# Down-projection of batches 1 to 7 by Strassen's scheme: seven products of quarters, the weights' combinations partly streamed from memory

## The chip, the cores and the metric

The kernel runs on one core of a Trainium2 chip. The metric is the time of one execution in device microseconds (us). A core has a matrix engine (TensorE, in the rows PE; its weight loads are PEld), VectorE (DVE), ScalarE (ACT), GpSimd (POOL) and SyncE (SP), which here issues every DMA. Each engine works through its own instructions in their order, and engines wait for each other on semaphores.

## The reference

```python
def sm_attn(qq, kk, vv):                       # float32 throughout
    s = scale * qq @ kk.T                      # scale = 1/sqrt(64)
    a = exp(s - max(s)); a = a / (sum(a) + 1e-9)
    return a @ vv
p_packed = sm_attn(p, k, v)                    # q, k, v: (8, 8, 576, 64), p: (8, 8, 32, 64)
out = sm_attn(q, p_packed, p_packed)
x = out.transpose(0, 2, 1, 3).reshape(8 * 576, 512)
h = x @ w_in                                   # w_in: (512, 2048)
g = h * tanh(softplus(h))                      # the Mish function
return g @ w_out                               # w_out: (2048, 512)
```

The weights arrive as float64 and are turned into float32 words in the kernel.

## The kernel before

The program handles the eight batches of 576 tokens in turn. Of a batch, 512 tokens ("MAIN") are done in four pieces of 128, and the last 64 ("REST") are kept aside in `g_rest`.

The hidden size 2048 is cut into 16 groups `f` of 128. A group has an *up* part (`Group.up`, matmuls on L707): for each half of the tokens, 288 columns, six matmuls add into a bank `ps_h`. It is six because the values are kept as a high and a low word (`aT_hi`, `aT_lo`, `wp_hi`, `wp_lo`, type fp32r), of which three products are taken, for two halves of the heads. ScalarE applies Mish (`mish`, L728, L730), VectorE splits the result into `g_hi` and `g_lo` (`halves`, L739, L740), and the *down* part (`down_one`, L744 to L746) multiplies it with the matching 128 rows of `w_out`. Its three matmuls (high by high, high by low, low by high) write 512 columns into one of four banks `acc`, once for each 128 tokens. The four banks gather over the 16 groups and are then copied out by ScalarE and VectorE in turn (L751, L753) and stored. The rest tokens of two batches fill one more set of 128 columns, done in `down_rest` (`ps_rest`) through the same lines.

The up weights are not `w_in` itself: `packed_w` multiplies `w_in` by the packed values `ppT` of the batch (L625, a plain float32 product of which TensorE makes two instructions) and splits the result (L636, L637), for 4 groups at a time. All of `w_in` (`wi`) and both words of `w_out` (`wo_hi`, `wo_lo`) stay in SBUF.

The attention of batch b+1 runs beside the projections of batch b, one piece at each `advance`: keys and queries turned (L430), scores (L440, L456 to L460), two exponentials (L468, L301), sums and division (L306 to L315), transposes back and the split (L333 to L339). Batch 0 is different: while it runs, weights are still loaded and converted by ScalarE, GpSimd and VectorE (L594 to L611), and its down-projection is plain float32 (L764).

The order on TensorE is the order of the code. On the other engines it is the code's order up to the end of batch 0 (`by_hand.close()` at `t == NF`); after that a scheduler in the compiler orders them. In the loop, `LAG = 2` puts the down part of a group two groups behind its up part.

Of the kernel before, what the change touches and what calls it, by code (L numbers as in the profile page):

```python
# [13 lines left out]
ALU = mybir.AluOpType  # L14
AX = mybir.AxisListType

LAG = 2
GB = 3
KVB = 8
KQB = 5  # L20
# [3 lines left out]
OB = 2  # L24
ATTENTION = {0: 4, 1: 2}
LOAD0 = 0
LOADS = {0: 1, 2: 1, 4: 1, 5: 1, 6: 1}
LATER = 12
FLOATS = 4
HALFWAY = 8  # L30
SPLIT0 = 14

# [7 lines left out]
def body(  # L40
# [54 lines left out]
    wi = [[const.tile([P, 2, 2, QC], F32, name=f"wi{c}_{g}") for g in range(2)] for c in range(DF // FC)]  # L95
# [4 lines left out]
    wo, wo_hi, wo_lo = {}, {}, {}  # L100

    def wo_slot(dtype, name):
        return wts.tile([P, DO], dtype, name=name, tag="wo", bufs=NF + 1)

    def split_wo(i):
        if i < HALFWAY:
            wo_hi[i], wo_lo[i] = [late[0].tile([P, DO], F32R, name=f"wo_{x}{i}") for x in ("hi", "lo")]
        else:
            wo_hi[i], wo_lo[i] = wo_slot(F32R, "wo_hi"), wo_slot(F32R, "wo_lo")
        both = [  # L110
            nc.scalar.copy(out=wo_hi[i], in_=wo[i]),
            nc.vector.tensor_tensor(out=wo_lo[i], in0=wo[i], in1=wo_hi[i].bitcast(F32), op=ALU.subtract),
        ]
        if i >= NF - SPLIT0:
            for x in both:
                tc.keep_in_program_order(x)
# [53 lines left out]
    class Batch:  # L170
# [12 lines left out]
        def start(self, pool):  # L183
            self.ppT = moe.tile([P, 2, P], F32, name="ppT")
            self.aT_hi = moe.tile([P, 2, S], F32R, name="aT_hi", tag="aT_hi")
            self.aT_lo = moe.tile([P, 2, S], F32R, name="aT_lo")
# [44 lines left out]
        def turn_weights(self, g, pool, by=(None, None)):  # L231
            self.a1T[g] = early.tile([R, 2, NI, P], F32, name="a1T", bufs=2)
# [46 lines left out]
        def match(self, g, pool):  # L279

            s2 = scores(pool, self.ppT[:, g, :], self.qT[g])
            if g == 0:
                self.a2 = moe.tile([P, 2, S // NP, NP], F32, name="a2", tag="aT_hi")
# [26 lines left out]
        def divide(self, gs, half=None):  # L310
# [4 lines left out]
            nc.vector.tensor_tensor(  # L315
# [7 lines left out]
        def back(self, g, halves=1):  # L323
            if self.b or g == 0:
                self.at = att.tile([P, S], F32, name="at", bufs=1)
            else:
                self.at = att.tile([P, S], F32, name="at", tag="T", bufs=2)
# [7 lines left out]
        def upper(self, g):  # L335
            nc.scalar.copy(out=self.columns(self.aT_hi[:, g, :]), in_=self.turned_back(g))

        def lower(self, g):
            nc.vector.tensor_tensor(  # L339
# [7 lines left out]

        def weigh(self, gs):
            self.share(gs)
            for g in range(gs.start, gs.stop):  # L350
                self.back(g)
                self.upper(g)
                self.lower(g)
# [18 lines left out]
    class Later(Batch):  # L372
# [39 lines left out]
        def start(self):  # L412
            self.ppT = moe.tile([P, 2, P], F32, name="ppT")
            self.aT_hi = moe.tile([P, 2, S], F32R, name="aT_hi", tag="aT_hi")
            self.aT_lo = moe.tile([P, 2, S], F32R, name="aT_lo")
# [8 lines left out]
        def pinned(self, x):  # L424
            if self.b == 2:
                tc.keep_in_program_order(x)
# [63 lines left out]
        def values(self, g):  # L490
# [11 lines left out]
            pending.append(lambda: (self.normalize(g, pp_ps), load_next()))  # L502
# [15 lines left out]
        def attention(self):  # L518


            self.by = "ACT" if self.b == 1 else None
            self.start()
            self.kT, self.qT = {}, {}
            for g in range(2):
                self.kT[g] = self.lanes(self.k_t[g])
                load_next()
                yield
            for g in range(2):
                self.score(g)
                yield  # L530
                flush()
                yield
            self.exps()
            for g in range(2):
                self.qT[g] = self.lanes(self.q_t[g])
                load_next()
                yield
            yield from self.turn_weights()
            self.sums(self.exped)
            yield  # L540
            for g in range(2):
                self.values(g)
                yield
            for g in range(2):
                self.turned(g)
            yield
            self.a2 = att.tile([P, 2, S // NP, NP], F32, name="a2", tag="a", bufs=1)
            for g in range(2):
                self.match(g)
                yield  # L550
                flush()
                yield
            both = slice(0, 2)
            self.peak(both)
            yield
            self.rise(both)
            yield
            self.share(both)
            for g in range(2):
                self.back(g)  # L560
                yield
                self.upper(g)
                yield
# [12 lines left out]
    class Weight:  # L576
# [6 lines left out]
        def fetch(self):  # L583
# [5 lines left out]
            self.dst = wi[self.n // 2][self.g][:, self.n % 2].rearrange("p m x -> p (m x)")  # L589
# [23 lines left out]
    class WeightOut(Weight):  # L613
# [3 lines left out]
        def fetch(self):  # L617
            self.st = stg.tile([P, 2 * FC], I32, name="w_st")
            nc.sync.dma_start(out=self.st, in_=w_out_v[:, self.i, :])
            self.dst = wo[self.i] = wo_slot(F32, "wo32")  # L620
# [12 lines left out]
    def part(ps):  # L633
# [405 lines left out]
```

## Time and profile before

| | |
|---|---|
| median of 3 runs | 750.88 us (750.29 to 751.61) |
| the profiled execution | 751.22 us, of which 749.4 us from its first to its last instruction (the span) |
| granted TensorE clock | 0.998 |
| busy: PE, PEld, DVE, ACT, POOL | 733.8, 563.7, 425.4, 296.1, 53.5 us |
| DMA | 56.34 MB, 31.7% of 16 engines' time |
| instructions | 12727 |

The times are microseconds unless ns is written. L744 is line 744 of the kernel. A row of the timeline gives the start, the length, the engine and line, what is written and read, and in brackets an idle time before it with what ended it. A group's row gives its count, its busy time, the mean length of one, and the idle time before them. Lengths of matmuls overlap: two rows that follow each other are read by their starts.

### The profile page before, as it was taken

The numbers are of one execution on the slowest core, as the hardware profiler recorded it, in microseconds if no ns is written. First come the engines' busy times: TensorE is split into PE (matmuls) and PEld (weight loads), VectorE is DVE, ScalarE is ACT, GpSimd is POOL, SyncE is SP. The second block draws the span as 40 slices with busy tenths as digits, with TensorE's granted clock in tenths as the row PEclk, the third lists the DMA queues.
The fourth block names the chain that finished last, engine by engine and source line by source line (L and its number), as shares of the span: only waits on it lengthen the run. The fifth ranks groups of instructions, "written<-read, shape, count | busy, mean of one in ns | idle before, by whom it ended". The sixth has DMA issues, their size and how long they took to land.

```text
span 749.4 us, 12727 instructions
## 1 busy us (share of the span) xinstructions
PE 733.8 (98%) x5160; PEld 563.7 (75%) x5160; DVE 425.4 (57%) x729; ACT 296.1 (40%) x691; POOL 53.5 (7%) x70
## 2 busy tenths in 40 slices
PE   8899999999999999999999999999999999999997
PEld 7545554688787878887787878877788778888886
DVE  3999767765846466554835557372843737332332
ACT  3776746452532433242522514243333424232221
POOL 0485440000000000000000000000000000000000
PEclk9999999999999999999999999999999999999999
DMA  9999960544204440143302342052201100010002
GB/s 235 296 293 247 270 114 1 127 71 95 32 1 111 64 95 1 59 69 72 56 1 80 62 96 32 15 106 41 56 1 42 29 2 1 1 57 1 0 1 71
DMA packets 186602, 56.34 MB, mean 75 GB/s; under 512 B 173488, under 2 KB 175792, under 8 KB 186544
## 3 DMA queue, kind: packets, MB, share of 16 engines
q1 hardware_dynamic: 186544, 55.53, 31.7%
q8 instruction: 41, 0.67, 0.4%
q14 instruction: 17, 0.14, 0.1%
HBM read 46.07 MB, written 9.44 MB: 74 GB/s over the span
## 4 chain that ended last, share of the span: by engine, by line
PE 91%; ACT 4%; DVE 3%; issue 1%; POOL 0%; DVEq 0%; ACTq 0%; POOLq 0%
PE ps_h L707 25%; PE acc L744 15%; PE acc L746 14%; PE acc L745 14%; PE acc L764 6%; PE ps_w L625 4%; PE ps_s L440 3%; PE ps_rest L746 2%; PE ps_rest L745 2%; PE ps_rest L744 2%; PE ps_pp L495 2%; PE ps_warm L828 1%; PE ps_a L482 1%; ACT wround L595 1%; PE ps_h L719 1%
## 5 line engine op out<-in xcount | busy, mean ns | idle before, releaser
L728 ACT ACTIVATE g<-ps_h 128x288 f32<-128x288 f32 (+1 forms) x256 | 97.3, 385 | 315.2 <-PE ps_h L707 283.4
L744 PE MATMUL acc<-wo_hi,g_hi 128*128 128x512 f32 x448 | 183.4, 409 | 0.0
L746 PE MATMUL acc<-wo_hi,g_lo 128*128 128x512 f32 x448 | 176.5, 394 | 0.0
L745 PE MATMUL acc<-wo_lo,g_hi 128*128 128x512 f32 x448 | 176.2, 393 | 0.0
L707 PE MATMUL ps_h<-aT_hi,wp_hi 128*128 128x288 f32 x496 | 157.5, 318 | 0.7 <-ACT g L728 0.7
L707 PE MATMUL ps_h<-aT_lo,wp_hi 128*128 128x288 f32 x496 | 146.1, 295 | 0.0
L707 PE MATMUL ps_h<-aT_hi,wp_lo 128*128 128x288 f32 x496 | 145.7, 294 | 0.0
L739 DVE CAST g_hi<-g 128x512 fp32r<-128x512 f32 x112 | 47.5, 424 | 163.1 <-ACT g L728 162.9
L744 PEld LDWEIGHTS acc<-wo_hi,g_hi 128*128 128x128 f32 x448 | 83.9, 187 | 43.1 <-issue 27.0
L707 PEld LDWEIGHTS ps_h<-aT_hi,wp_hi 128*128 128x128 f32 x496 | 93.1, 188 | 16.2 <-issue 3.8
L707 PEld LDWEIGHTS ps_h<-aT_lo,wp_hi 128*128 128x128 f32 x496 | 93.2, 188 | 14.7 <-issue 5.5
L746 PEld LDWEIGHTS acc<-wo_hi,g_lo 128*128 128x128 f32 x448 | 84.0, 188 | 19.7
L707 PEld LDWEIGHTS ps_h<-aT_hi,wp_lo 128*128 128x128 f32 x496 | 93.1, 188 | 0.0
L745 PEld LDWEIGHTS acc<-wo_lo,g_hi 128*128 128x128 f32 x448 | 84.2, 188 | 8.7
L740 DVE TENSOR_TENSOR g_lo<-g,g_hi 128x512 fp32r<-128x512 f32 x112 | 77.3, 690 | 6.1 <-DVE g_hi L739 0.5
L764 PE MATMUL acc<-wo,g 128*128 128x512 f32 x128 | 64.3, 607 | 3.4 <-ACT g L728 2.7
L637 DVE TENSOR_TENSOR wp_lo<-ps_w,wp_hi 128x512 fp32r<-128x512 f32 x56 | 36.1, 683 | 16.7 <-ACT wp_hi L636 16.7
L636 ACT CAST wp_hi<-ps_w 128x512 fp32r<-128x512 f32 x56 | 30.1, 591 | 31.0 <-PE ps_w L625 31.0
L625 PE MATMUL ps_w<-wi,ppT 64*32 64x512 f32 (+1 forms) x576 | 38.7, 553 | 1.9 <-DVE wi L611 1.9
L764 PEld LDWEIGHTS acc<-wo,g 128*128 128x128 f32 x128 | 21.3, 189 | 22.0 <-issue 11.5
L730 ACT ACTIVATE g_rest<-ps_h 128x64 f32<-128x64 f32 x128 | 28.3, 221 | 0.0
L746 PE MATMUL ps_rest<-wo_hi,r_lo 128*128 128x512 f32 x64 | 25.1, 393 | 0.0
(116 smaller groups left out, 739.1 us busy)
## 6 DMA issues: line engine op xcount, KB each, us to landing
w_st<-in_moe_w_in_dram SPq DMA_DIRECT2D x16, 512.0 KB, 8.1
w_st<-in_moe_w_out_dram SPq DMA_DIRECT2D x16, 512.0 KB, 7.0
k_n<-in_k_dram SPq DMA_DIRECT2D x56, 144.0 KB, 3.3
q_n<-in_q_dram SPq DMA_DIRECT2D x56, 144.0 KB, 3.2
v_n<-in_v_dram SPq DMA_DIRECT2D x56, 128.0 KB, 2.8
out_dram<-o SPq DMA_DIRECT2D x28, 256.0 KB, 2.0
k_t<-in_k_dram SPq DMA_DIRECT2D x4, 288.0 KB, 4.9
v_t<-in_v_dram SPq DMA_DIRECT2D x4, 288.0 KB, 6.9
```

The source lines that it names most:

```text
L625: nc.tensor.matmul(out=ps[h * NP:(h + 1) * NP, :], lhsT=ppTb[row:row + D, g, h * NP:(h + 1) * NP], rhs=w[row:row + D], start=True, stop=Tr ...
L636: nc.scalar.copy(out=hi, in_=ps)
L637: nc.vector.tensor_tensor(out=lo, in0=ps, in1=hi.bitcast(F32), op=ALU.subtract)
L707: nc.tensor.matmul(out=ps, lhsT=w[:, fs], rhs=a[:, g, cs], start=(n == 0), stop=(n == 5))
L728: nc.scalar.activation(out=self.act[:, hf * HALF:hf * HALF + m], in_=ps[:, :m], func=AF.Mish)
L730: nc.scalar.activation(out=self.g_rest[self.b % 2][self.f // 4][:, self.f % 4, :], in_=ps[:, m:], func=AF.Mish)
L739: nc.vector.tensor_copy(out=hi, in_=self.act)
L740: nc.vector.tensor_tensor(out=lo, in0=self.act, in1=hi.bitcast(F32), op=ALU.subtract)
L744: nc.tensor.matmul(out=acc, lhsT=hi[:, cs], rhs=wh, start=start, stop=False)
L745: nc.tensor.matmul(out=acc, lhsT=hi[:, cs], rhs=wl, start=False, stop=False)
L746: nc.tensor.matmul(out=acc, lhsT=lo[:, cs], rhs=wh, start=False, stop=stop)
L764: nc.tensor.matmul(out=accs[c], lhsT=grp.act[:, cs], rhs=wo[f], start=f == 0, stop=f == NF - 1)
```

## The change

Batch 0 stays as it was but for where its weights lie. From batch 1 on, the down-projection is made for 256 tokens at a time (a `Unit`: half of MAIN of one batch, or the rest tokens of four batches), over pairs `j` of groups, 256 rows of `w_out`. Each pair is a 2 by 2 product of quarters: tokens by hidden rows (128 by 128) and hidden rows by output columns (128 by 256). Seven products take the place of eight (`PRODUCTS`), each as three matmuls of the two words, 256 columns wide, into seven of the eight halves of four banks. What it needs beside them:

- `Step.sums`: four sums of the activations, three instructions on GpSimd (L770 to L774). `Step.halves`: both words of seven quarters, two copies on ScalarE (L781) and two subtractions on VectorE (L782), into `x_hi`, `x_lo` (two buffers).
- `combine`: for each `j` the seven combinations of the weights in two words (1.8 MB), made by GpSimd, ScalarE and VectorE at the end of batch 0 (`j` = 0, 1) and during batch 1 (2 to 7). Four stay in SBUF; `j` = 1, 3, 5, 7 (`STREAMED`) are written to DRAM and brought back into two slots (`bring`, two for each pass). `w_in` is written to DRAM too (`wi_saved`) and comes back by halves (`fetch_in`).
- `Unit.close`: the seven halves become the output by one copy on ScalarE and seven additions on VectorE (L812, L822).
- `packed_half` makes the up weights for 2 groups at a time, in 56 calls for batches 1 to 7.

The loop after batch 0 is new. For each batch an "up" pass makes for each `j` the up parts of both halves of the tokens (256 and 320 columns) and the down step of the first half; a "down" pass does the down steps of the second half, kept in `g_half`; after batches 3 and 7 a "rest" pass follows. A down step is put one place behind (`queue`, `drop`). Tables (`BESIDE`) say beside which step each piece of the next attention stands (a letter for the place and the step's number: `d1` is behind the second step of a down pass), and from batch 2 on the division moves to GpSimd. `by_hand.close()` moves to the end, so every engine now follows the code's order.

```diff
+    def combine(j):
...
+        for out, x, y, op in (
+            (t[:, 0], b1[:, 1], b1[:, 0], ALU.subtract),
+            (t[:, 1], b2[:, 1], t[:, 0], ALU.add),
+            (t2[:, 0], b1[:, 1], b2[:, 1], ALU.add),
+            (t2[:, 1], t[:, 1], b2[:, 0], ALU.subtract),
+        ):
+            keep(nc.gpsimd.tensor_tensor(out=out, in0=x, in1=y, op=op))
+        for k, src in ((slice(0, 1), b1[:, 0:1]), (slice(1, 3), b2), (slice(3, 5), t), (slice(5, 7), t2)):
+            if k.start < 3:
+                nc.scalar.copy(out=w[:, k, 0], in_=src)
+            else:
+                nc.gpsimd.tensor_copy(out=w[:, k, 0], in_=src)
+            (nc.gpsimd if k.start == 5 else nc.vector).tensor_tensor(
+                out=w[:, k, 1], in0=src, in1=w[:, k, 0].bitcast(F32), op=ALU.subtract
+            )
+        if j in STREAMED:
+            nc.sync.dma_start(out=w_saved[j], in_=w.bitcast(F32))
...
+            k, src = (slice(0, 3), self.raw[:, 1:4]) if part == 0 else (slice(3, 7), self.s)
+            nc.scalar.copy(out=self.hi[:, k], in_=src)
+            nc.vector.tensor_tensor(
+                out=self.lo[:, k], in0=src, in1=self.hi[:, k].bitcast(F32), op=ALU.subtract
+            )
...
+            for x, k, bank, u in PRODUCTS:
+                out = self.unit.banks[bank][:, u]
+                for i, (l, m) in enumerate(((self.hi, 0), (self.hi, 1), (self.lo, 0))):
+                    nc.tensor.matmul(
...
+        for turn, (kind, b) in enumerate(passes):
+            if kind == "up":
...
+                for i, j in enumerate(orders[turn]):
...
+                    up_pair(b, j, 0, raw)
+                    st = Step(a, j, raw)
+                    st.sums()
...
+                    aside("a", i)
...
+                        st.halves(0)
...
+                        drop(wait=True)
...
+                        st.halves(1)
+                    queue.append(lambda st=st, i=i: st.down(i))
...
+                            pack()
+                        close()
+                    else:
+                        early = Step(later, orders[turn + 1][0], stored[orders[turn + 1][0]])
+                        early.sums()
+                        early.halves(0)
+                        early.halves(1)
+                        aside("b", i)
+                        drop()
+                    up_pair(b, j, 1, stored[j])
...
+                    aside("c", i)
...
+            for i, st in enumerate(steps):
...
+                    steps[i + 1].sums()
+                if st is not early:
+                    st.halves(0)
+                    st.halves(1)
+                if queue:
+                    drop()
+                queue.append(lambda st=st, i=i: st.down(i))
...
+                if i == NJ - 2 and b + 1 < B:
+                    pack()
+                aside("d", i)
```

On TensorE, in the middle of a batch, two of a group's four down parts and the up part behind them stood like this (the names left of the arrow are banks):

```order
L744 MATMUL acc_3395<-wo_hi,g_hi 128x512
L745 MATMUL acc_3395<-wo_lo,g_hi 128x512
L746 MATMUL acc_3395<-wo_hi,g_lo 128x512
L744 MATMUL acc_3396<-wo_hi,g_hi 128x512
L745 MATMUL acc_3396<-wo_lo,g_hi 128x512
L746 MATMUL acc_3396<-wo_hi,g_lo 128x512
L707 MATMUL ps_h<-aT_hi,wp_hi 128x288
```

Now a step of a down pass begins with these rows, and the next step follows without an up part between them:

```order
L793 MATMUL acc_6306<-w,x_hi 128x256 x2
L793 MATMUL acc_6306<-w,x_lo 128x256
L793 MATMUL acc_6306<-w,x_hi 128x256 x2
L793 MATMUL acc_6306<-w,x_lo 128x256
L793 MATMUL acc_6308<-w,x_hi 128x256 x2
L793 MATMUL acc_6308<-w,x_lo 128x256
```

A bank takes two products of three matmuls, and the low word is read by the third of each. On ScalarE, around the second exponential of a batch's attention (`a`, line L301, before):

```order
L728 ACTIVATE g<-ps_h 128x288
L301 ACT_TABLE_LOAD
L301 ACTIVATE a_4703<-a_4703 128x1152
L728 ACT_TABLE_LOAD
L728 ACTIVATE g<-ps_h 128x224
L730 ACTIVATE g_rest_4689<-ps_h 128x64
L636 CAST wp_hi<-ps_w_4822 128x512
```

The same exponential (now L351) stands at the end of an up pass, with the words of the last step (`g`) and of the next pass's first step (`g_half`) ahead of it, and the copy that begins to empty the banks (L812) behind it:

```order
L781 CAST x_hi<-g 128x384
L781 CAST x_hi<-s 128x512
L781 CAST x_hi<-g_half 128x384
L781 CAST x_hi<-s 128x512
L351 ACT_TABLE_LOAD
L351 ACTIVATE a_7164<-a_7164 128x1152
L812 COPY o<-acc_6727 128x256
L751 ACT_TABLE_LOAD
L751 ACTIVATE g_half<-ps_h 128x256
```

On VectorE, where a batch's banks were emptied and beside its attention, before:

```order
L739 CAST g_hi<-g 128x512
L740 TENSOR_TENSOR g_lo<-g,g_hi 128x512
L753 COPY o<-acc_3397 128x512
L787 TENSOR_TENSOR o_rest<-ps_rest,o_rest 128x512
L456 TENSOR_REDUCE mx<-ps_s_4329 128x1
```

Now, at the change from an up to a down pass:

```order
L782 TENSOR_TENSOR x_lo<-s,x_hi 128x512
L822 TENSOR_TENSOR o<-acc_6727,o 128x256
L822 TENSOR_TENSOR o<-acc_6729,o 128x256 x3
L822 TENSOR_TENSOR o<-acc_6728,o 128x256 x2
L822 TENSOR_TENSOR o<-o,acc_6730 128x256
L782 TENSOR_TENSOR x_lo<-g_half,x_hi 128x384
L782 TENSOR_TENSOR x_lo<-s,x_hi 128x512
L356 TENSOR_REDUCE sm_7500<-a_7164 128x36
```

Seven additions now stand between two steps' low words, where single copies stood, and behind the second step stands the first piece of the softmax's division.

More of the change, by code (lines that the diff above doesn't have):

```diff
@@ L15 @@
 AX = mybir.AxisListType
-LAG = 2
-GB = 3
 KVB = 8
-KQB = 5
+KQB = 4
 STB = 8
@@ L98, in body, with keep, bring @@
     late = []
[L100 to L107, printed above, removed]
-        else:
[L109 to L116, printed above, removed]
+    W = {}
+    def combine(j):
+        if j == 0:
+            W[j] = late[0].tile([P, NP7, 2, QC], F32R, name="w_first", bufs=1)
+        else:
+            W[j] = w_slot(F32R, "w")
+        w = W[j]
+        b1, b2 = (wo[2 * j + i].rearrange("p (u x) -> p u x", u=2) for i in range(2))
+        t, t2 = (wts.tile([P, 2, QC], F32, name="t", tag="o", bufs=OB) for _ in range(2))
+        def keep(x):
+            pass
+        for out, x, y, op in (
[15 more added lines that the diff above has]
+            nc.sync.dma_start(out=w_saved[j], in_=w.bitcast(F32))
+    def bring(j):
+        W[j] = w_slot(F32R, "w")
+        nc.sync.dma_start(out=W[j].bitcast(F32), in_=w_saved[j])
     w_in_v = w_in.bitcast(I32).rearrange("(m p) f -> p m f", p=P)
@@ L538, in attention @@
[L538 to L561, printed above, removed]
+            both = slice(0, 2)
+            def keys(g):
+                if g == 0:
+                    self.start()
+                self.kT[g] = self.lanes(self.k_t[g])
+            def queries(g):
+                self.qT[g] = self.lanes(self.q_t[g])
+            def match(g):
+                if g == 0:
+                    self.a2 = att.tile([P, 2, S // NP, NP], F32, name="a2", tag="a", bufs=1)
+                self.match(g)
@@ new lines, in project @@
+    def project(ps, b, wp, n, cs):
+        fs = slice(n * P, n * P + P)
+        aT_hi, aT_lo = batches[b].aT_hi, batches[b].aT_lo
+        n = 0
+        for g in range(2):
+            w_hi, w_lo = wp[g]
+            for w, a in ((w_hi, aT_hi), (w_hi, aT_lo), (w_lo, aT_hi)):
+                nc.tensor.matmul(out=ps, lhsT=w[:, fs], rhs=a[:, g, cs], start=(n == 0), stop=(n == 5))
+                n += 1
+    UNIT = 2 * P
+    PRODUCTS = ((0, 0, 0, 0), (5, 4, 0, 1), (3, 5, 2, 0), (4, 3, 2, 1), (2, 1, 1, 0), (6, 2, 1, 1), (1, 6, 3, 0))
@@ L748, in evac, with store_half, store, store_rest @@
+    def store_half(b, hf):
+        def store(c, o):
+            c += 2 * hf
+            for dst, lo, hi in batches[b].rows(c):
+                nc.sync.dma_start(out=dst, in_=o[lo:hi, :])
+        return store
+    def store_rest(q):
+        def store(c, o):
+            for i in range(2):
+                dst = batches[4 * q + 2 * c + i].rest_rows()
+                nc.sync.dma_start(out=dst, in_=o[i * REST:(i + 1) * REST, :])
+        return store
+    accs = []
     def evac(acc, c):
-        o = wts.tile([P, DO], F32, name="o", bufs=OB)
+        o = late[0].tile([P, DO], F32, name="o0", tag="g_half", bufs=NJ)
@@ L1015 @@
+        while queue:
+            drop()
+        by_hand.close()
 _INS = ["q", "k", "v", "p", "moe_w_in", "moe_w_out"]
```

465 lines of the change are left out of this document (283 added, 182 removed), and 6 rows, old and new, of tables (BESIDE, BESIDE1).

## Prediction

> **What bounds the kernel now.** I read the page first: its busy times, the chain that ended last and the granted clock.
>
> ```profile
> PE 733.8 (98%) x5160; PEld 563.7 (75%) x5160; DVE 425.4 (57%) x729; ACT 296.1 (40%) x691; POOL 53.5 (7%) x70
> PE 91%; ACT 4%; DVE 3%; issue 1%; POOL 0%; DVEq 0%; ACTq 0%; POOLq 0%
> core 0: 749.4 us, clock 0.998
> ```
>
> TensorE is busy for 98% of the span at the full clock and makes 91% of the chain. An average hides stages, so I asked for stretches; the first below runs from batch 3's first up matmul to batch 5's, the second from batch 7's to the end.
>
> ```profile
> core 0: us, PE busy (x) PEld busy (x) DVE busy (x) ACT busy (x) POOL busy (x), PEclk, DMA share, GB/s
> 304.58:479.82 175.24, 175.24 (x1258) 139.81 (x1256) 96.20 (x168) 62.50 (x147) 0.00 (x0) 1.00 0.28 56
> 655.04:749.40 94.36, 89.63 (x502) 74.41 (x500) 29.32 (x53) 22.95 (x66) 0.00 (x0) 0.99 0.07 26
> ```
>
> In the middle TensorE has no idle time at all: two batches take 175.2 us, 87.6 each, DVE is busy 55% of it, ACT 36%, GpSimd not once. So less matmul work shortens the kernel, as long as nobody makes TensorE wait. What a matmul costs is the distance of starts, from the timeline:
>
> ```profile
> 400.07 0.40 PE L744 MATMUL acc<-wo_hi,g_hi 128*128 128x512 f32 x1
> ...
> 401.47 0.29 PE L707 MATMUL ps_h<-aT_hi,wp_hi 128*128 128x288 f32 x1
> ...
> 402.26 0.39 PE L744 MATMUL acc<-wo_hi,g_hi 128*128 128x512 f32 x1
> ```
>
> Six down matmuls of 512 columns lie between the first two rows: 1.40/6 = 0.233 us each. Six of 288 columns follow: 0.79/6 = 0.132.
>
> **The change on TensorE.** Groups of the whole run give the counts (each stands for one of three lines):
>
> ```profile
> L744 PE MATMUL acc<-wo_hi,g_hi 128*128 128x512 f32 x448 | 183.4, 409 | 0.0
> L744 PE MATMUL ps_rest<-wo_hi,r_hi 128*128 128x512 f32 x64 | 25.1, 392 | 0.0
> 141.45 0.19 PEld L744 LDWEIGHTS acc<-wo_hi,g_hi 128*128 128x128 f32 x1 [0.84 <-DVE xT L430]
> 141.56 0.19 PEld L745 LDWEIGHTS acc<-wo_lo,g_hi 128*128 128x128 f32 x1
> ```
>
> Removed are 3 x (448 + 64) = 1536 matmuls of 512 columns, 357.9 us at 0.233. Added are 16 units x 8 steps x 21 = 2688 of 256 columns, whose price no row shows. The straight line through 288 and 512 columns gives 0.117. From below, two weight loads stand as close as 0.11 (the last two rows), and every matmul needs one; from above, 0.132 is the shortest full matmul seen. I take the line: 2688 x 0.117 = 314.5, a gain of 43.4 (62 and 3 at the two ends). The up parts go from 288 + 288 to 256 + 320 columns, the same sum, at no cost. The up weights are made in 56 halves instead of 28 wholes:
>
> ```profile
> 298.06 0.39 PE L746 MATMUL acc<-wo_hi,g_lo 128*128 128x512 f32 x1
> 298.38 1.09 PE L625 MATMUL ps_w<-wi,ppT 64*32 64x512 f32 x16
> 299.40 0.50 PE L744 MATMUL acc<-wo_hi,g_hi 128*128 128x512 f32 x1
> 299.73 0.39 PE L745 MATMUL acc<-wo_lo,g_hi 128*128 128x512 f32 x1
> 50.08 0.66 PE L625 MATMUL ps_w<-wi,ppT 64*32 64x256 f32 x16
> 50.67 1.13 PE L764 MATMUL acc<-wo,g 128*128 128x512 f32 x2
> ```
>
> From 298.06 to 299.73 pass 1.67 us, of which two matmuls are 0.47: a whole costs 1.20, of it 1.02 its own. A half is 0.59 of its own (50.08 to 50.67), with the same 0.18 around it 0.77: 56 x 0.77 - 28 x 1.20 = +9.5. Together TensorE's work falls by 33.9 us. Shared over batches 1 to 7 that is under 5 us a batch, so about 4 us of new waits in each would use it up.
>
> **The waits that the change adds.** A down step of 21 matmuls lasts 2.46 us, and before it can end ScalarE, VectorE and GpSimd must have made the next step's operands. Their prices (the first five also show the price by size):
>
> ```profile
> L740 DVE TENSOR_TENSOR g_lo<-g,g_hi 128x512 fp32r<-128x512 f32 x112 | 77.3, 690 | 6.1 <-DVE g_hi L739 0.5
> L739 DVE CAST g_hi<-g 128x512 fp32r<-128x512 f32 x112 | 47.5, 424 | 163.1 <-ACT g L728 162.9
> L658 DVE TENSOR_TENSOR wp_lo<-ps_w,wp_hi 128x256 fp32r<-128x256 f32 x12 | 4.5, 413 | 3.5 <-ACT wp_hi L657 3.5
> L111 ACT CAST wo_hi<-wo 128x512 fp32r<-128x512 f32 x16 | 10.1, 630 | 0.0
> L728 ACT ACTIVATE g<-ps_h 128x288 f32<-128x288 f32 x128 | 52.7, 412 | 114.8 <-PE ps_h L707 86.1 <-issue 20.9 <-ACT wp_hi L636 7.2
> L301 ACT ACT_TABLE_LOAD x7 | 9.0, 1283 | 0.1
> L301 ACT ACTIVATE a<-a 128x1152 f32<-128x1152 f32 x7 | 8.2, 1167 | 1.7 <-DVE a L295 1.6
> L306 DVE TENSOR_REDUCE sm<-a 128x36 f32<-128x1152 f32 x7 | 9.4, 1349 | 5.6 <-ACT a L301 5.6
> L333 DVE STREAM_TRANSPOSE at<-a 128x576 f32<-128x576 f32 x15 | 11.6, 774 | 0.2
> L339 DVE TENSOR_TENSOR aT_lo<-at,aT_hi 128x576 fp32r<-128x576 f32 x16 | 12.5, 781 | 4.6 <-ACT aT_hi L336 4.6
> L430 DVE STREAM_TRANSPOSE xT<-k_n 128x1152 f32<-128x1152 f32 x14 | 18.6, 1337 | 0.0
> 67.96 0.62 POOL L600 TENSOR_SCALAR wsign<-wo 128x512 f32<-128x512 f32 x1
> 34.83 0.94 POOL L600 TENSOR_SCALAR wsign<-wi 128x512 f32<-128x512 f32 x1
> 34.19 1.10 DVE L606 SCALAR_TENSOR_TENSOR wi<-wi,wsign 128x512 int32<-128x512 int32 x1
> ```
>
> For ScalarE I use 0.63 for 512 elements and 0.52 for 384 (between that and the 0.41 of 288), for VectorE 0.69 and 0.55 (between L658 and L740). GpSimd has only one-input rows, 0.62 for 512. Two inputs cost at least that and at most twice; VectorE's own step from one input to two (424 to 690 ns) is the nearest row, so 1.0. `sums` then is 1.0 plus the overhead of two more instructions, some 0.5: 1.5 us (0.9 to 2.2).
>
> In a plain down step this fits: 0.52 + 0.63 + 0.69 = 1.84 us after its buffer is free, under 2.46, and since the low word is read only by a product's third matmul there are five matmuls, 0.58 us, more. Four places do not fit, in each of batches 1 to 6:
>
> 1. The last step of an up pass has only one down step (2.46) between its Mish and its own products, where the others have weights and an up part as well. Drain 0.16 (a matmul's row of 0.29 less its 0.132), Mish 0.39 (256 columns, a little under L728's 288), sums 1.5, high words 0.63 and low words 0.69 are 3.4; TensorE can wait until 2.46 + 0.58 = 3.04. With a brush against a VectorE instruction (0.62 grew to 0.94) I take 0.8 (0 to 2).
> 2. Then all four banks must be emptied before the next pass's first product. ScalarE has a table load and an exponential, 1.28 + 1.17, ahead of its copy, and behind it stand seven additions of 256 columns at about 0.4. The next step's sums end near 3.9 (counted from the last Mish's columns, with the brush), its high words at 4.55, table and exponential at 7.0; the last product ends at 2 x 2.46 + 0.8 = 5.7, so the copy begins 1.3 us behind it. The up part behind that covers 1.75; the first bank is free at 2.1, the second at 3.3, the third at 4.1, while TensorE wants them at 1.75 and, once it has the one, 0.7 later the next: 0.35 + 0.5 + 0.1, so 1.0 (0 to 2).
> 3. In the down pass VectorE has the attention between two steps' low words: 1.9 for the sums at `d1` (1.35 and two small ones), 1.55 for the transposes at `d3`, 1.56 for the split at `d4`, and `d3` waits for the division on GpSimd, 1152 elements, 2.25 at the price above. Of each step VectorE has 2.46 - 0.69 - 0.55 = 1.2 to spare. Over the spare: 0.7, 0.35 and some 0.75 for the division, 0.4: 2.2 (0 to 5).
> 4. At the start of an up pass the banks of the scores come free only when VectorE, behind a 1.34 us turning of keys, has read them (0.35), and after the first exponential ScalarE is a table load and 1.2 us behind when TensorE wants a bank for the turned weights (0.75): 1.1 (0.3 to 2.5).
>
> With 0.3 for the small ones this is 5.4 a batch, 32.4 for six; before, the middle of the kernel shows no idle time that could be set against it. Batch 7 has no attention beside it: 1.4. In batch 1 GpSimd has six `combine` more, each four sums of 256, two copies and one subtraction of 512, some 5 us, and a step's sums queue behind it, ScalarE behind those, and the up weights behind ScalarE: 4 in all (0 to 15). Each of two rest passes starts without an up part to hide the emptying: 2.0. At the end, one addition after the last matmul becomes a copy and seven: 2.5.
>
> Batch 0's new work I cost at nothing. `combine` for `j` = 0 and 1 and the 4.2 MB of `w_in` that go to DRAM stand in its last five groups, 95 to 130 us, where GpSimd runs dry and the queue, in slices of 18.7 us, too:
>
> ```profile
> DMA  9999960544204440143302342052201100010002
> ```
>
> If the loads end later there, the writes fall into batch 1, beside the combinations that are costed above.
>
> Sum: 751.2 (the profiled execution, the span's 749.4 and 1.8 around it) - 33.9 + 32.4 + 1.4 + 4.0 + 2.0 + 2.5 = 759.6. The median shown is 0.3 lower than that execution, which leaves 759.3, say 759, with 748 to 770 for this case alone.
>
> [...]
>
> **Streaming.** The seven products' weights of one `j` are 128 x 14,336 bytes, 1.8 MB, two for each pass.
>
> ```profile
> 0.00:30.00 30.00, 25.02 (x323) 20.95 (x324) 17.41 (x41) 13.07 (x30) 3.28 (x11) 1.00 0.97 294
> ```
>
> At the 294 GB/s of the filled queue one takes 6.2 us. The second is issued after a pass's third step and read by its eighth, in a down pass 4 to 5 steps (about 12 us) later, when both have had 12.5: just in time, and the waits above add room. I cost it at nothing; that cover ends if attention loads go ahead of it. SP issues in order, and a `bring` waits for its slot's last product; what is queued behind it, loads and stores for the pass after, has a pass of time.
>
> **Rivals.**
> - *TensorE stays the bound, and the kernel is faster.* GpSimd's place decides it: if its two-input instruction costs hardly more than the one-input row, sums take 1.0, places 1 and 3 fall to about a third, batch 1's queue to 1, and with engines that start an instruction 0.1 us before the last has ended, waits are near 2 a batch: 751.2 - 33.9 + 12 + 1 + 1 + 2 + 2.5 - 0.3 = 735. It decides where the waits stay below 4.0 a batch ((33.9 - 1.4 - 4 - 2 - 2.5)/6). For it speaks that VectorE and ScalarE are half idle in the middle; against it that the waits lie at few places where averages do not help.
> - *GpSimd and VectorE block each other.* Beside each other, 0.62 became 0.94 and 0.69 became 1.10 (rows above). If each of a step's instructions pays that, sums are 2.2, the waits 8.5 a batch and batch 1's 15: 759 + 19 + 11 = 789. [...]
> - *The streamed weights come late,* 2.5 us in each of nine down and rest passes: 759 + 22 = 781.
> - *Weight loads bound the short matmul* at 0.132: 759 + 40 = 799.
>
> **How the numbers follow.** A difference of 0.2%, 1.5 us, is about what a measurement of this kernel can tell from none. Forecast 0.43 (of it 0.05 within 0.2%, 0.38 slower), rival one 0.39, two 0.10, three 0.05, four 0.03. So faster 0.39, same 0.05, slower 0.56. The predicted time is 759. The range must reach into both signs: 728, some way under rival one, to 787, which leaves out the rest of the second and the fourth.
>
> **What would show it.** Starts of the 256-column matmuls 0.117 apart show the first term, 0.13 the fourth rival. Idle time of TensorE ended by VectorE's low words at the end of up passes, by the additions that empty the banks, and by VectorE in the third to sixth step of down passes, some 5 us a batch, would show the second term; a TensorE at 98% again shows the first rival. GpSimd's three sums over 2 us, with VectorE's subtractions over 1 us beside them, show the second; waits that a DMA of `w` ended show the third. I am wrong if GpSimd's price is wrong, or if the spare time of a step is larger than sums of full lengths make it.

## The result, and the profile after

The changed kernel takes 784.9 us in the median of four executions (782.19 to 788.10), the kernel before, beside it, 751.1: a ratio of 1.045 (95% interval 1.041 to 1.049). Slower, as forecast, but by 34 us and not by 8. The executions differ in the clock that TensorE was granted: 0.987 in the fastest, which is the profiled one, 0.980 in the slowest.

The page of the profiled execution, its busy times, its chain and its clock:

```profile
PE 726.5 (93%) x6760; PEld 614.2 (79%) x6760; DVE 519.4 (67%) x873; ACT 414.4 (53%) x969; POOL 375.3 (48%) x516
PE 62%; DVE 14%; ACT 10%; POOL 7%; issue 4%; DMA 2%; SPq 1%; DVEq 0%; ACTq 0%; POOLq 0%
core 0: 780.5 us, clock 0.987
```

TensorE's share of the chain fell from 91% to 62%; VectorE, ScalarE and GpSimd now hold 31% of it. By stretches, first of the kernel before (batch 1, batch 2), then of the changed one (batch 1, batch 2, batches 4 and 5, batch 7 with its rest pass):

```profile
129.81:219.68 89.87, 88.79 (x627) 69.33 (x626) 59.74 (x104) 39.36 (x91) 0.00 (x0) 1.00 0.36 68
219.68:304.58 84.90, 84.90 (x618) 67.64 (x616) 47.02 (x82) 29.65 (x70) 0.00 (x0) 1.00 0.30 60
```

```profile
130.81:227.74 96.93, 82.59 (x793) 71.59 (x792) 74.47 (x111) 49.94 (x122) 71.95 (x91) 0.96 0.75 222
227.74:313.06 85.32, 80.85 (x815) 71.12 (x814) 55.81 (x98) 46.71 (x110) 33.99 (x49) 1.00 0.69 196
420.82:592.74 171.92, 163.70 (x1627) 145.04 (x1625) 108.40 (x191) 92.46 (x218) 66.96 (x98) 0.98 0.67 190
678.55:774.12 95.57, 94.64 (x831) 89.36 (x829) 47.36 (x87) 45.21 (x114) 49.84 (x72) 1.00 0.43 162
```

The columns are length, then busy PE, PEld, DVE, ACT and POOL, clock, DMA share and rate. Batch 1 grew by 7.1 us. A plain batch takes 85.3 to 86.0, although the rest rows, which before lay among the batches, now have passes of their own (batch 3 with the first of them takes 107.8). In a plain batch VectorE is busy 55.8 us and GpSimd 34.0, together more than the batch is long. These busy times include the time for which the two engines hold each other up: in the rows below, low words of 0.69 us alone take 2.61 beside GpSimd's division.

Who kept TensorE waiting, over the whole kernel:

```profile
PE acc L793 <- DVE x_lo L782: 14.8, 17, 2.4
PE acc L793 <- DVE o L822: 7.9, 12, 1.0
PE ps_h L740 <- ACT g_rest L753: 4.3, 3, 2.1
PE acc L793 <- ACT x_hi L781: 2.7, 7, 0.4
...
PE acc L793 <- DMA w<-w_saved: 0.3, 1, 0.3
```

The low words lead; the streamed weights, with 0.3 us, are as good as absent. The longest wait for low words, from the timeline of batch 5's down pass (GpSimd, VectorE, TensorE):

```profile
575.68 2.34 POOL L365 TENSOR_TENSOR a<-a,sm 128x1152 f32<-128x1152 f32 x1
575.45 0.58 DVE L782 TENSOR_TENSOR x_lo<-g_half,x_hi 128x384 fp32r<-128x384 f32 x1
575.96 2.61 DVE L782 TENSOR_TENSOR x_lo<-s,x_hi 128x512 fp32r<-128x512 f32 x1
578.50 0.55 DVE L782 TENSOR_TENSOR x_lo<-g_half,x_hi 128x384 fp32r<-128x384 f32 x1
578.63 0.39 PE L793 MATMUL acc<-w,x_lo 128*128 128x256 f32 x1 [1.91 <-DVE x_lo L782]
```

VectorE's low words, 0.69 us alone, begin during GpSimd's division and end half a microsecond behind it. The stall can then cost a second time, through TensorE's clock. Three stretches: what follows the same stall in batch 2, then the stall in batch 5 and what follows it:

```profile
299.80:303.50 3.70, 3.70 (x33) 3.70 (x33) 3.70 (x6) 1.86 (x4) 3.40 (x5) 1.00 0.96 403
576.40:578.90 2.50, 0.59 (x5) 0.38 (x4) 2.50 (x2) 0.27 (x1) 1.87 (x2) 1.00 1.00 169
578.90:582.60 3.70, 3.70 (x20) 3.70 (x20) 2.67 (x5) 0.58 (x2) 3.39 (x6) 0.54 0.89 360
```

Behind the one in batch 5 TensorE was granted 0.54 of its clock and did 20 matmuls in the time in which it did 33 in batch 2.

To see where the time went I took, from batch 1's first matmul (129.81 before, 130.81 after) to the last one, the distances of neighbouring matmul starts in both traces, and set against each the undisturbed distance of its kind (0.1175, 0.147, 0.2325 and 0.132 us for 256, 320, 512 and 288 columns). What lies above falls into short gaps (0.03 to 0.2 us), stalls (over 0.2) and runs of four or more at half speed:

| us, batch 1 to the last matmul | before | after | difference |
|---|---|---|---|
| undisturbed up and down matmuls | 534.3 | 493.5 | -40.8 |
| packs of up weights, their own time | 29.0 | 32.6 | +3.6 |
| short gaps | 14.2 (150) | 28.6 (302) | +14.4 |
| stalls | 2.6 (5) | 48.5 (60) | +45.9 |
| low clock | 0 | 6.6 (70 matmuls) | +6.6 |
| attention, batch 0's last matmuls, rounding | 34.3 | 33.2 | -1.1 |
| sum | 614.4 | 643.0 | +28.6 |

With 1.0 in batch 0, and 1.6 from the last matmul's end to the span's end, less 0.1 since the last matmul is shorter, that is the spans' difference of 31.1.

### The profile page after: what moved, and what is told of

It reads as the page before. It is cut to its first block, busy times and chain, and to the rows that moved or that the text cites. A ratio compares the mean times of both kernels' runs of the same rounds, so it can differ in the third digit from the quotient of the medians.

```text
span 780.5 us, 17209 instructions
## 1 busy us (share of the span) xinstructions
PE 726.5 (93%) x6760; PEld 614.2 (79%) x6760; DVE 519.4 (67%) x873; ACT 414.4 (53%) x969; POOL 375.3 (48%) x516
## 4 chain that ended last, share of the span: by engine, by line
PE 62%; DVE 14%; ACT 10%; POOL 7%; issue 4%; DMA 2%; SPq 1%; DVEq 0%; ACTq 0%; POOLq 0%
PE acc L793 27%; PE ps_h L740 20%; DVE x_lo L782 5%; PE ps_w L658 4%; PE acc L855 4%; DVE o L822 2%; PE ps_s L481 2%; POOL s L773 2%; POOL s L770 2%; PE ps_pp L536 1%; DMA w<-w_saved 1%; POOL t L154 1%; ACT L509 1%; POOL s L774 1%; ACT a L509 1%
## 5 line engine op out<-in xcount | busy, mean ns | idle before, releaser
L793 PE MATMUL acc<-w,x_hi 128*128 128x256 f32 x1568 | 291.1, 286 | 5.7 <-ACT x_hi L781 2.7
L793 PEld LDWEIGHTS acc<-w,x_hi 128*128 128x128 f32 x1568 | 243.8, 192 | 21.6 <-issue 9.1
L793 PE MATMUL acc<-w,x_lo 128*128 128x256 f32 x784 | 224.7, 287 | 15.0 <-DVE x_lo L782 14.3
L770 POOL TENSOR_TENSOR s<-g 128x256 f32<-128x256 f32 x56 | 41.9, 748 | 273.5 <-ACT g L751 273.5
L740 PE MATMUL ps_h<-aT_hi,wp_hi 128*128 128x256 f32 (+1 forms) x496 | 165.3, 333 | 4.3 <-ACT g_rest L753 4.3
L793 PEld LDWEIGHTS acc<-w,x_lo 128*128 128x128 f32 x784 | 150.2, 192 | 19.8 <-DVE x_lo L782 19.6
L782 DVE TENSOR_TENSOR x_lo<-s,x_hi 128x512 fp32r<-128x512 f32 x128 | 112.4, 878 | 54.0 <-ACT x_hi L781 54.0
L740 PE MATMUL ps_h<-aT_hi,wp_lo 128*128 128x256 f32 (+1 forms) x496 | 146.9, 296 | 0.8 <-DVE wp_lo L684 0.8
L740 PE MATMUL ps_h<-aT_lo,wp_hi 128*128 128x256 f32 (+1 forms) x496 | 147.0, 296 | 0.0
L781 ACT CAST x_hi<-s 128x512 fp32r<-128x512 f32 x128 | 79.7, 622 | 93.2 <-POOL s L774 93.2
L782 DVE TENSOR_TENSOR x_lo<-g,x_hi 128x384 fp32r<-128x384 f32 x56 | 36.3, 648 | 58.1 <-ACT x_hi L781 58.1
L855 PE MATMUL acc<-home,g 128*128 128x512 f32 x128 | 63.4, 605 | 2.1 <-ACT g L729 1.5
L770 POOL TENSOR_TENSOR s<-g_half 128x256 f32<-128x256 f32 x56 | 46.1, 824 | 33.4 <-ACT g_half L751 18.9
L781 ACT CAST x_hi<-g_half 128x384 fp32r<-128x384 f32 x56 | 28.9, 516 | 56.3 <-PE acc L793 51.8
```

The costliest lines, as they stand in the source:

```text
L740: nc.tensor.matmul(out=ps, lhsT=w[:, fs], rhs=a[:, g, cs], start=(n == 0), stop=(n == 5))
L770: e.tensor_tensor(out=s[:, 0:2], in0=r[:, 0:1].to_broadcast([P, 2, P]), in1=r[:, 1:3], op=ALU.subtract)
L781: nc.scalar.copy(out=self.hi[:, k], in_=src)
L782: nc.vector.tensor_tensor(out=self.lo[:, k], in0=src, in1=self.hi[:, k].bitcast(F32), op=ALU.subtract)
L793: nc.tensor.matmul(out=out, lhsT=l[:, x], rhs=w[:, k, m], start=(n == 0 and i == 0 and u == 0), stop=(n == NJ - 1 and i == 2), skip_group_ ...
L855: nc.tensor.matmul(out=accs[c], lhsT=grp.act[:, cs], rhs=wo[f], start=f == 0, stop=f == NF - 1)
```

## The experiments

All ratios are to the kernel before, run beside it on the same chip (750.6 to 751.3).

**Who divides.** `by=nc.vector` for all batches.

```
-"div": lambda: self.divide(both, by=nc.gpsimd if self.b > 1 else nc.vector)
+"div": lambda: self.divide(both, by=nc.vector)
```

> Edit: the division of the second attention weights of batches 2 to 7 goes from GpSimd to VectorE. Theory A (GpSimd and VectorE hold each other up for a whole instruction): in the changed kernel VectorE's low words at 575.96, 0.51 us long elsewhere, took 2.61 beside GpSimd's division of 2.34, and TensorE waited 2.1 us; the division on VectorE is 1.36 (its 1152-element subtraction of the same shape), so the stall in the third step of a down pass falls to about 1 us, the low granted clock behind it (0.54 for 3.7 us, in batches 4 to 6) goes, and the time is 772 to 778. Theory B (VectorE simply has too much to do between the steps of a down pass, whoever divides): 1.36 us more on VectorE's queue lengthens the stall, 785 to 790. Theory C (streamed weights): no change, 785.

Measured: 778.9 us, 1.037 (1.035 to 1.039). Batch 5 went from 85.9 to 84.5 us, no run at half speed is left in batches 2 to 6, and TensorE's waits for low words fell:

```profile
PE acc L793 <- DVE x_lo L782: 8.1, 24, 2.4
```

VectorE took on the work itself and TensorE still gained 6 us: theory A, though 0.9 above its range. (The 0.51 us named there is the shortest row of 384 elements; low words of 512 take 0.69 alone.) In the profiled executions 4.3 us of the gain are matmuls no longer at half clock (clock 0.995 against 0.987) and 4.6 are shorter stalls, while short gaps grew by 2.8. What is left in a down pass, five stalls of 0.3 to 0.4 us, still ends with VectorE's low words.

**Division in pieces.**

```
+for i in range(4):
+    a, m = a2[:, 9 * i:9 * i + 9], sm[:, 9 * i:9 * i + 9]
+    nc.gpsimd.tensor_tensor(out=a, in0=a, in1=m..., op=ALU.mult)
```

> Edit: GpSimd's division of batches 2 to 7 as four instructions of 288 elements instead of one of 1152; the work and the engine stay. Theory A (whole instructions exclude each other): VectorE's low words wait for one piece of some 0.6 us and not for 2.3, so the 2.61 us low words become about 1.1, the stall of 2.1 us in the third step of a down pass falls below 1, the low clock behind it goes, and the time is 774 to 780, near the division on VectorE (778.9). Theory A2 (the two only share bandwidth, each slowed in proportion to the time they overlap): the same overlap, low words still above 2 us, 784 to 787.

Measured: 782.9 us, 1.043 (1.041 to 1.045). GpSimd's four pieces, and the low words beside them:

```profile
577.47 3.99 POOL L375 TENSOR_TENSOR a<-a,sm 128x288 f32<-128x288 f32 x4
577.74 1.16 DVE L792 TENSOR_TENSOR x_lo<-s,x_hi 128x512 fp32r<-128x512 f32 x1
578.82 1.02 DVE L792 TENSOR_TENSOR x_lo<-g_half,x_hi 128x384 fp32r<-128x384 f32 x1
579.77 1.16 DVE L792 TENSOR_TENSOR x_lo<-s,x_hi 128x512 fp32r<-128x512 f32 x1
```

The low words came out as A has it: 2.61 became 1.16, and the stall in the third step 0.6 instead of 2.1. But beside VectorE's instructions the four pieces took 3.99 together, where the division in one took 2.34, and each of the next low words was held as well (1.0 to 1.2); the stalls of the fifth and sixth steps are 0.4 to 0.7, where the division on VectorE leaves 0.3 to 0.4. A's time was missed by 3 us. A plain batch takes 85.4 us, where it takes 84.5 with VectorE dividing and 85.9 in the changed kernel: most of the two engines' time was only dealt out in other portions. A2 falls, since it had the low words above 2 us.

**The sums on VectorE, alone and with the division.**

```
-SUMS = nc.gpsimd
+SUMS = nc.vector
```

> Edit: the three sums of each step go from GpSimd to VectorE. On GpSimd they take 2.0 to 2.5 us from the first start to the last end; on VectorE, by its row of 0.41 for 256 elements, about 1.0. Theory A: the low words come back from 0.88 to 0.69 us, the wait at the end of an up pass (1.1 us) goes, and in batch 1 a step's sums no longer queue behind 6.8 us of combinations on GpSimd; the division still blocks in the down pass: 768 to 776. Theory B: VectorE gets some 1.0 us more in each of 16 steps of a batch and has only about 1.2 to spare in a down step, so the third to sixth steps lose 1 us each: 785 to 800.

> Edit: both of the above; GpSimd then does nothing from batch 2 on, only the weights' combinations in batch 1. Theory A: the gains add, 758 to 766, with VectorE's low words at 0.69 us throughout. Theory B: VectorE has 1.36 + 1.0 us a step more between two low words at the place of the division: 790 to 805, and the stall in the third to fifth step grows.

Measured: 806.9 us, 1.075 (1.073 to 1.077), and 804.1 us, 1.070 (1.069 to 1.072). The groups of low words of the changed kernel, of the first and of the second:

```profile
L782 DVE TENSOR_TENSOR x_lo<-s,x_hi 128x512 fp32r<-128x512 f32 x128 | 112.4, 878 | 54.0 <-ACT x_hi L781 54.0
```

```profile
L782 DVE TENSOR_TENSOR x_lo<-s,x_hi 128x512 fp32r<-128x512 f32 x128 | 90.7, 708 | 6.3 <-ACT x_hi L781 6.3
```

```profile
L782 DVE TENSOR_TENSOR x_lo<-s,x_hi 128x512 fp32r<-128x512 f32 x128 | 89.6, 700 | 6.8 <-ACT x_hi L781 6.8
```

Without GpSimd's sums beside them the low words do come back to the row of before, and still the kernel with the sums alone on VectorE loses 22 us: theory B, but 7 us above its range; the one with both lies in its range. With the sums alone, batch 5 has VectorE busy for 66.3 of 88.6 us, in order, with low words behind sums behind attention; the stalls in the second and third steps of a down pass grew to 1.3 and 2.9, and the time lost at half clock from 6.6 to 11.9 over the whole kernel (clock 0.977 in the profiled execution, 0.987 in the changed kernel's), which the forecast did not count. GpSimd, for all that it holds up VectorE (low words of 878 ns in the mean with its sums, 708 without), is the better place for the sums.

**Streaming.**

```
 def bring(j):
-    W[j] = w_slot(F32R, "w")
-    nc.sync.dma_start(out=W[j].bitcast(F32), in_=w_saved[j])
+    W[j] = W[STREAMED[-1]]
```

> Edit: the 31 reloads of combined weights (1.8 MB each) are left out; the products of the streamed j then use the combination of the last one, so the output is another. Theory C (late or contending transfers cost time): 765 to 775. Theories A and B: the only wait that a transfer of w ended was 0.3 us, so 784 to 786, apart from what a different granted clock does.

Measured: 784.6 us, 1.044 (1.042 to 1.047). Some 56 MB (31 times 1.8) less to load, and nothing gained: theory C falls.

**Batch 1's combinations, left out, and lightened.**

```
 def combine(j):
+    if j > 1:
+        W[j] = W[j % 2]; return
```

> Edit: the six combinations of batch 1 are left out (products of j above 1 use those of 0 or 1, and the reloads bring the one stored combination), so the output is another. Theory E: batch 1 stalls 17.1 us and has a low clock for 2.4 more where batch 2 stalls 5.9; all 13 us of the difference are the combinations, 770 to 774. Rival (batch 1's own order of the attention and the full waits of a first batch): at most 5 us, 780 to 783.

Measured: 772.4 us, 1.029 (1.027 to 1.031). Batch 1 in that kernel:

```profile
130.20:215.45 85.25, 80.05 (x793) 70.37 (x792) 54.77 (x93) 46.06 (x110) 33.62 (x49) 0.98 0.67 192
```

It is 11.7 us shorter and like any other batch, as theory E has it. In the changed kernel GpSimd's queue shows why (the first combination, the next step's sums, and what waited):

```profile
135.27 0.72 POOL L154 TENSOR_TENSOR t<-home 128x256 f32<-128x256 f32 x1
...
140.52 1.60 POOL L160 TENSOR_TENSOR w<-t,w 128x512 fp32r<-128x512 f32 x1
142.09 0.74 POOL L770 TENSOR_TENSOR s<-g 128x256 f32<-128x256 f32 x1
```

A combination holds GpSimd for 6.8 us, a step's sums for 2.0, together 8.8; ScalarE, in order, waits for those sums with the up weights' words behind it, and TensorE stalls about 2 us in most of these steps (`PE ps_s <- DVE wp_lo` 2.2 in one of them).

```
-if k.start < 3: nc.scalar.copy(out=w[:, k, 0], in_=src)
-else: nc.gpsimd.tensor_copy(out=w[:, k, 0], in_=src)
+nc.scalar.copy(out=w[:, k, 0], in_=src)
```

> Edit: the two copies of 512 in each combination of weights (1.63 us on GpSimd) go to ScalarE, in batch 0 and batch 1. Theory E (GpSimd bounds batch 1: 6.8 us of combination and 2.0 of sums in each of six steps, 8.8 where a step otherwise takes 7.4): a step falls to about 7.4, so batch 1 (96.9 us) gets 6 to 8 us shorter, 776 to 780. Rival: the high words queue on ScalarE behind two more copies of 0.6 and nothing is gained, 783 to 787.

Measured: 782.4 us, 1.042 (1.040 to 1.044). A step of batch 1 fell from 8.8 to 7.8 us, not to 7.4, since GpSimd now waits 0.7 for ScalarE's copy before its last subtraction; and the last step of that up pass lost 3.5, partly at the low clock (0.96 over batch 1), in place of 1.5. Both forecasts missed: batch 1 as a whole stalls 14.8 instead of 17.1.

**The exponential behind the emptying, alone and with the division on VectorE.**

```
-"b7": "rise", "d1": "tally load", ...
+"d0": "rise", "d1": "tally load", ...
```

> Edit: in batches 2 to 6 the second exponential with its table load moves from the last step of the up pass to the first of the down pass, behind the copy and the seven additions that empty the banks. Theory D (place 2 of the prediction: ScalarE's copy stands 2.4 us behind table load and exponential): the waits for the additions (1.0 + 0.3 and about 0.3 around them) go in five batches, 775 to 779. Rival: the wait moves, since VectorE's tally, in order ahead of low words, then waits for the exponential: 783 to 790.

> Edit: the division on VectorE and the second exponential in the first step of the down pass, both together. If the wait that the late exponential made in the down pass (1.1 us where the one for the banks had been 1.6) is its own and adds to the division's: 776 to 779, the two gains added. If it came of the queue on VectorE in which the division now stands too: 780 to 786.

Measured: 783.1 us, 1.043 (1.041 to 1.046), and 778.9 us, 1.037 (1.035 to 1.039), the same as with the division alone. The waits for the emptying additions (7.9 us in the changed kernel) went, but for those of the first rest pass, and the low and high words of the second step came late instead:

```profile
575.42 0.50 PE L793 MATMUL acc<-w,x_hi 128*128 128x256 f32 x2 [0.96 <-ACT x_hi L781]
```

Table load and exponential now stand ahead of those high words. The stall moved by one step, as the rival has it. It even became shorter: all stalls of the profiled execution are 44.9 us, 3.6 less than in the changed kernel. But TensorE lost 11.8 us at half clock in place of 6.6 (clock 0.978 in the profiled execution, 0.987 in the changed kernel's). Together with the division on VectorE the time lies within the range for two gains that add, but that is luck: the median is that of the division alone, and a plain batch is only 0.3 us shorter (84.3 against 84.5).

**A third buffer for the words.**

In short, without the one call that filled the second buffer of `wi_s`:

```
-x_hi, x_lo: bufs=2;  OB = 3;  wi_s: bufs=2
+x_hi, x_lo: bufs=3;  OB = 2;  wi_s: bufs=1
```

> Edit: the division on VectorE, and three buffers instead of two for a step's high and low words (paid for by one buffer less of the up weights' source and of the output tiles). In a down pass the quarters of all steps are there from the start, so a third buffer lets ScalarE and VectorE run a step further ahead. Theory H (the stalls of the down pass are a lack of lead, VectorE has time enough over the whole pass): the 1.8 us left there and the rest passes' stalls go, 768 to 775. Rival (VectorE and GpSimd are short of time over the whole pass, so that a lead is used up at once): 777 to 782.

Measured: 795.9 us, 1.060 (1.058 to 1.062). The first two waits:

```profile
PE ps_w L658 <- DMA wi_s<-wi_saved: 15.2, 11, 3.4
PE acc L793 <- DVE x_lo L782: 8.1, 24, 2.4
```

What paid for the buffer cost 15 us (the up weights' source, with one buffer, lands too late), so the time says nothing on theory H. The second line speaks against H: 8.1 us in 24 waits, to the digit what the division on VectorE alone has. In this run a third buffer changed none of these waits.

**Without the work on the operands.** Sums, high and low words only in the first step; then the sums alone left out; then the low words alone.

```
 def halves(self, part):
+    if kept:
+        self.hi, self.lo = kept[0].hi, kept[0].lo; return
```

> Edit: only the first step makes its sums, high words and low words; all later steps multiply by that one's, so the output is another. The combinations, the division, the exponentials and the emptying of the banks stay. Theory F (TensorE's own work is what the prediction made it, less some 9 us of short gaps where a matmul follows a small one or a wait, and the rest of the loss is waiting for operands): the waits at the end of up passes and in the down passes, the low clock behind them and the queueing of sums in batch 1 go, some 20 + 6 + 8 us and a few in the rest passes; the waits for the emptied banks stay: 740 to 752. Rival G (short matmuls, their weight loads and the gaps between are what costs): no faster than 770.

> Edit: the sums are made once, by the first step; the high and low words of every later step are still made each time, of those first sums, so the output is another. GpSimd then has the division and batch 1's combinations only. In a plain batch of 85.9 us VectorE is busy 55.5 and GpSimd 33.4, together 88.9. Theory J (the sums are the dear part, by their own 2.0 to 2.5 us and by what they take from VectorE): the wait at the end of up passes goes, of the down pass only the division's stall stays, sums no longer queue in batch 1: 745 to 755. Theory K (VectorE, in order, with the low words behind the attention): more than half of the 48 us remains, 762 to 775.

> Edit: the low words are made once, by the first step; sums and high words are made each time, so the output is another. VectorE has some 22 us less to do in each batch and GpSimd's sums have it beside them less often. Theory J: the sums' own length keeps ScalarE's high words late, 755 to 770. Theory K: 740 to 752. If both of the two experiments come out near 745, neither is the bound by itself but their sum, that is the chain of sums, high words and low words, or the time that the two engines share.

Measured: 737.0 us, 0.981 (0.979 to 0.983); 759.9 us, 1.014 (1.011 to 1.017); 754.5 us, 1.005 (1.003 to 1.007). Batches 4 and 5 of the three (the second kernel's profiled execution took 764.9, its slowest):

```profile
400.52:557.19 156.67, 156.67 (x1627) 141.06 (x1625) 62.72 (x129) 59.71 (x154) 4.27 (x2) 1.00 0.72 208
```

```profile
414.05:580.33 166.28, 161.80 (x1627) 144.45 (x1626) 101.16 (x191) 90.99 (x218) 4.45 (x2) 0.98 0.69 196
```

```profile
408.65:570.61 161.96, 158.96 (x1626) 141.57 (x1625) 64.58 (x129) 92.58 (x218) 58.99 (x98) 1.00 0.69 200
```

Theory F, though 3 us below its range: 48 us of the 785 come of making the operands, that is the waits for them and the low clock and short gaps behind these waits, and without it the kernel is faster than the one before, as the first term had it. Rival G, no faster than 770, falls. Sums alone are 25 of the 48, low words alone 30, together more than 48. Neither run fell into a theory's range (759.9 lies between 755 and 762, 754.5 between 752 and 755), and neither theory stands by itself: what costs is both in one chain, or the time that the two engines share, and these runs don't tell those two apart. What is left without sums is, in a plain batch, mostly the division's stall (2.0). In all three a new wait appears, three times, 5.1 to 5.7 us in all, for `w` from memory: the streaming was free only behind the other waits.

No variant that does the whole computation came under the kernel before; the best was the division on VectorE, 1.037. But for the one exponential, no run changed the places of the attention's pieces between the steps, so whether another order of the same work would do better stays open.

## Why the prediction was wrong, step by step

The steps that failed are three terms of what is added to TensorE's own work: short gaps (nothing forecast, 9.0 us), the low clock (nothing, 6.6) and the queue in batch 1 (4.0 forecast, 11.7 measured). Together they miss by 23.3 of the 25.6 us, and what the other terms miss nearly cancels.

- *What bounds it.* Right that TensorE bounds the kernel before and that under 5 us of waits a batch would use the gain up.
- *0.117 for a matmul of 256 columns.* Right; from the timeline, three of them in 0.35 us:

```profile
561.20 0.40 PE L793 MATMUL acc<-w,x_hi 128*128 128x256 f32 x2
561.43 0.28 PE L793 MATMUL acc<-w,x_lo 128*128 128x256 f32 x1
561.55 0.39 PE L793 MATMUL acc<-w,x_hi 128*128 128x256 f32 x2
```

  With 0.1175 and 0.2325 the term is -41.3 (forecast -43.4). The up parts cost 0.3 more, the packs of up weights +9.0 (3.6, and 28 more pairs of gaps of 0.1; forecast 9.5).
- *Short gaps.* No term. 9.0 us more than the packs bring. Some 4.9 of them stand right behind stalls (46 gaps), and 3.5 at 23 places like this one, the second of two up groups that now follow each other:

```profile
685.57 0.28 PE L740 MATMUL ps_h<-aT_hi,wp_lo 128*128 128x256 f32 x1
685.73 0.19 PEld L740 LDWEIGHTS ps_h<-aT_hi,wp_hi 128*128 128x128 f32 x1
685.73 0.39 PE L740 MATMUL ps_h<-aT_hi,wp_hi 128*128 128x256 f32 x1
```

  The weight load, which at the matmul before runs under the one ahead (from 685.45 for the matmul at 685.57), starts here only with its own, which is 0.39 instead of 0.28 long; why it waits, no row shows.
- *5.4 us of waits a batch.* The sum was right: batches 2 to 6 stall 27.7 us, 27.0 were forecast. Its parts: place 1 took 1.0 (0.8 forecast), place 2 1.7 (1.0), place 3 2.4 to 3.0 (2.2), place 4 0.3 (1.1). That the sum fits so well is in part luck: place 4 makes up for the others, and place 3 had another cause than the sum of lengths given for it, since the low words were held for the whole of GpSimd's division (2.61 us beside its 2.34).
- *`sums` 1.5 us.* Too low: 2.0 to 2.5 from first start to last end, as the second rival had it. That two inputs cost at most twice the one-input row of 0.62 was an estimate; the subtraction into 512 words took 1.6.
- *Batch 1, 4.0 for the combinations.* Of the terms that the sum had, the one that failed most: 17.1 us of stalls where 5.4 + 4.0 were forecast, 7.7 more. The queue that it named (sums behind the combination, ScalarE behind the sums, the up weights behind ScalarE) is the one that the rows of batch 1 show, but its size was wrong: a combination is 6.8 us on GpSimd and not 5, and GpSimd's 8.8 a step became the step.
- *The granted clock.* No term, since the middle of the kernel before showed 1.00; it cost 6.6 us, behind stalls that the change brought.
- *Streaming, batch 0, batch 7 and rest passes, tail.* 0, 1.0, 3.5 and 1.6 against 0, 0, 3.4 and 2.5.

The misses: first term and up parts 2.4, packs -0.5, short gaps 9.0, places 0.7, batch 1 7.7, clock 6.6, batch 7 and rest 0.1, batch 0 1.0, tail -0.9; less 2.6 of stalls that the kernel before had; and the median lies 2.7 above the profiled execution where 0.3 below was assumed, 3.0. Together 26.5; with the table's sixth line (-1.1) and the shorter last matmul (-0.1) 25.3, against 784.9 - 759.3 = 25.6.

So the second rival was the nearest in its mechanism (789, from sums of 2.2, 8.5 us a batch and 15 in batch 1), and 0.10 was too little for it. That its number came so near is in part luck: a batch stalls 5.2 to 5.9 us and not 8.5, and the short gaps and the low clock, which it did not have either, make up for that. The third rival's 781 lies as near by number, but leaving out the streaming gained nothing. The two rows of the kernel before, 0.62 to 0.94 and 0.69 to 1.10, already showed the two engines holding each other up, and VectorE's 48 us a batch before and the 26 that the prediction's own prices give GpSimd (16 x 1.5 + 2.25) should have been added: 74 of 88 leaves little room for two engines that wait for each other. Low words of 2.61 beside a division of 2.34, and of 1.16 beside pieces of it, where 0.69 is their length alone, showed it again.

## What to carry to other kernels

A change that trades matmul time for work on operands is priced by the chain of engines that makes them: add VectorE's and GpSimd's times where they run side by side (here 55.8 and 34.0 in a batch of 85.3), and look at each long instruction of the one as a possible stall of the other (here the division of 2.34 us, which held low words for 2.61). A stall of TensorE of 2.1 us could cost some 1.5 more through the clock (20 matmuls in the time of 33), and closely packed short matmuls lost a tenth of a microsecond behind a stall (46 gaps, 4.9 us). Moving a wait's cause by a step moved the wait, and one more buffer left it as it was. Moving the one long instruction from GpSimd to VectorE helped; moving the many short ones there cost 22 us.

## What the hardware did that I had not expected

- A stall of 2.1 us sufficed for the clock to fall to half for 2.1 to 3.4 us of matmuls (70 in five such runs, 6.6 us), but not each time: of five equal stalls in batches 2 to 6 three were followed by it. The clock of the trace tells them apart. Its five stretches at half between matmuls start at 155.66, 210.27, 493.58, 578.91 and 664.24, are 3.41 us long each, and lie 16, 83, 25 and 25 times 3.413 us apart. Cut by that distance from these starts, here are the stretch with the stall and the one behind it, in batch 2 and in batch 5:

```profile
295.59:299.01 3.42, 1.93 (x15) 1.52 (x13) 3.35 (x5) 1.03 (x2) 3.25 (x3) 1.00 1.20 196
299.01:302.42 3.41, 2.84 (x24) 2.84 (x25) 3.41 (x5) 0.78 (x2) 2.66 (x4) 1.00 0.91 370
575.50:578.91 3.41, 1.36 (x9) 0.95 (x9) 3.41 (x4) 1.03 (x2) 2.73 (x3) 1.00 1.03 172
578.91:582.32 3.41, 3.41 (x18) 3.41 (x18) 2.62 (x4) 0.30 (x1) 3.12 (x5) 0.50 0.86 345
```

  In batch 2 the stall reaches over the end of its stretch, in which TensorE is busy for 1.93 us of 3.41, and the clock stays; in batch 5 it lies within one, 1.36 are busy, and the clock is halved. In the two other batches with a halved clock 1.49 and 1.66 were busy, in the other without one 1.87. That is what five stalls show; what sets the clock, no row shows.
- Batch 1, the same in five of the kernels, took 96.8 to 100.1 us, with stalls alike (16.4 to 17.3 us) and 2.3 to 4.6 us lost at half clock (clock 0.96 to 0.93): some of the spread between executions lies there.
- GpSimd's two-input instruction took 0.74 us for 256 elements and 0.46 for 128, so by an estimate from these two some 0.18 us and 2.2 ns an element; the division of 1152 took 2.13 to 2.35, less than that line gives, and the subtraction into 512 rounded words 1.6, more than it gives.
